# Attention on one Trainium2 core: loads by group, jumps over rarely used code, and a reordered last group

## The chip, the cores and the metric

The kernel runs on one core of a Trainium2 chip. A core has five engines with a queue of instructions each: PE multiplies matrices, ACT applies functions such as exp, DVE and POOL do element-wise work, and SP issues the transfers here. Engines wait for one another through semaphores. The metric is the device time of one execution in microseconds (us), lower is better; the kernel before takes 543.33 us, the median of 14 runs from 542.11 to 545.58.

## The reference: softmax attention with shared keys

```python
B, Hq, Hkv, Sq, Sk, D = 16, 32, 8, 288, 512, 128     # bfloat16, values of about 0.05
k = jnp.repeat(k, Hq // Hkv, axis=1)
v = jnp.repeat(v, Hq // Hkv, axis=1)
scores = jnp.einsum("bhqd,bhkd->bhqk", q, k) * D ** -0.5
out = jnp.einsum("bhqk,bhkd->bhqd", _softmax(scores, axis=-1), v)
```

Four query heads share one key and value head, so the work falls into 16 x 8 = 128 groups, each with 4 x 288 = 1152 query rows against 512 keys.

## The kernel before

A *group* (`g`, of `NG` = 128) is one key head of one batch: R = 1152 query rows in NT = 9 tiles of 128, 512 keys in NJ = 4 tiles. Scores are made with the keys on the partitions, so one group has NJ x R = 4608 score columns, cut into NC = 3 *chunks* of CH = 1536 columns (three PSUM banks). A *step* is one chunk. There are 384 of them. For step n:

- **S** (`op_s`, L416): PE multiplies the transposed k by the transposed q into one of two score buffers in PSUM (`ps_s`). `pieces` (L410) cuts a chunk where a bank or a key tile ends, so a chunk takes four matmuls.
- **E** (`op_exp`, L456): ACT takes exp of the chunk, without subtracting a maximum, into `pt_sb` in bfloat16.
- **PV** (`op_pv`, L437): PE multiplies three query tiles of the group by v, four key tiles each, twelve matmuls of 129 columns into one of two PSUM banks (`ps_o`). The 129th column of v holds ones, so it collects the sum of the exps. Chunks run over keys first, so PV of a group needs all three exps of the group.
- **Evacuation** (`op_rc` and `op_ev`, L478 and L485): DVE takes the reciprocal of three sums and multiplies three output tiles by them into `o_sb`, a ring of six groups.

PE's order is written out: S of step n, then PV of step n - LAG, with LAG = 4; after the last S the last four PV follow one another. S of step n waits for E of n - 2, PV of step r for the evacuation of r - 2.

SP issues all transfers, in an order sorted by due times counted in steps. Loads come by *unit* of UG = 4 groups (`op_load`, L379), three units deep: one transposing transfer of k, one transposing transfer of q, and a plain one of v into `vd_sb`. POOL copies v from there into `v_sb`, beside the column of ones, once per unit (`op_vc`, L467). In the first unit, k and q of group 0 come by themselves (`part=0`), then those of groups 1 to 3 (`part=1`), then v of all four. A group's output is stored in one transfer (`op_store`, L403), which waits for the group's last evacuation.

Because no maximum is subtracted, the kernel ends with a test. DVE keeps the largest and smallest reciprocal of each batch (`op_stat`, L500), reduces them at the end (L560, L562), compares them with limits (L563, L566), PE sums the verdicts over the partitions (L534), and DVE writes an integer `flag_i` (L569). Then `guarded` (L578) lets each engine load the flag (L582) and branch (L583): where the flag isn't zero, a general version of the attention (`general_path`, L17) runs from the start. With these inputs it is skipped. The general code of each engine stands between that branch and the end of the program, where all engines drain and meet (L324).

Of the kernel before, what the change touches and what calls it, by code (L numbers as in the profile page):

```python
# [284 lines left out]

def bass_standalone__gqa_softmax__near_ridge_kernel(
# [16 lines left out]
    CB = 3  # L303
    CH = CB * BANK
    COLS = NJ * R
    NC = COLS // CH
    assert COLS % CH == 0 and NT % 3 == 0 and NC == NT // 3
    scale = float(D) ** -0.5
    DV = D + 1
    VP = DV  # L310
# [3 lines left out]
    NSLOT = 3  # L314
    NPT = 3
    NO = 6

# [6 lines left out]
    with ExitStack() as es:  # L324
# [8 lines left out]
        block = es.enter_context(nc.Block())  # L333
        main = ExitStack()
        vd_sb = main.enter_context(nc.sbuf_tensor("vd_sb", [P, NSLOT, UG, NJ * D], BF16))
        v_sb = main.enter_context(nc.sbuf_tensor("v_sb", [P, NSLOT, UG * NJ, VP], BF16))
        qt_sb = main.enter_context(nc.sbuf_tensor("qt_sb", [P, NSLOT, NT, UG, P], BF16))
# [5 lines left out]
        ck_sb = main.enter_context(nc.sbuf_tensor("ck_sb", [P, 4], FP32))  # L343
# [26 lines left out]
        for name in ["s_one", "s_s", "s_e", "s_pv", "s_rc", "s_ev", "s_stat", "s_bad", "s_flag", "s_go", "s_q0", "s_k0", "s_vc"]:  # L370
            S(name)
        for i in range(NSLOT):
            for name in ["s_q%d", "s_k%d", "s_v%d"]:
                S("u" + name % i)
        for i in range(NO):
            S("s_o%d" % i)


        def op_load(u, part=None):  # L379
            eng = nc.sync  # L380
            sl = u % NSLOT
            if u >= NSLOT:
                last = (u - NSLOT + 1) * UG - 1
                for (s, n) in need(eng, [("s_s", NC * (last + 1))]):
                    eng.wait_ge(s, n)
            g0, g1 = {None: (0, UG), 0: (0, 1), 1: (1, UG)}[part]
            sq = sem["s_q0"] if part == 0 else sem["us_q%d" % sl]
            sk = sem["s_k0"] if part == 0 else sem["us_k%d" % sl]
            gg = u * UG
            eng.dma_start_transpose(  # L390
                kt_sb[:, sl, :, g0:g1].rearrange("d j g p -> d j (g p)"),
                k_v[(gg + g0) * P:(gg + g1) * P]).then_inc(sk, 16)
            eng.dma_start_transpose(  # L393
                qt_sb[:, sl, :, g0:g1].rearrange("d t g p -> d t (g p)"),
                q_v[(gg + g0) * P:(gg + g1) * P]).then_inc(sq, 16)
            if part != 0:
                if u >= NSLOT:
                    for (s, n) in need(eng, [("s_vc", u - NSLOT + 1)]):
                        eng.wait_ge(s, n)
                eng.dma_start(  # L400
                    vd_sb[:, sl], v_v[:, gg:gg + UG]).then_inc(sem["us_v%d" % sl], 16)

        def op_store(g):  # L403
            eng = nc.sync
            for (s, n) in need(eng, [("s_ev", NC * (g + 1))]):
                eng.wait_ge(s, n)
            eng.dma_start(o_v[g], o_sb[:, g % NO].rearrange("p t d -> p (t d)")).then_inc(sem["s_o%d" % (g % NO)], 16)


        def pieces(i):  # L410
            cuts = sorted({i * CH, (i + 1) * CH}
                          | {x for x in range(0, COLS, BANK) if i * CH < x < (i + 1) * CH}
                          | {x for x in range(0, COLS, R) if i * CH < x < (i + 1) * CH})
            return list(zip(cuts[:-1], cuts[1:]))

        def op_s(n):  # L416
            eng = nc.tensor
            g, i = n // NC, n % NC
            u, gi = g // UG, g % UG
            sl = u % NSLOT  # L420
            waits = []
            if g == 0:
                waits += [("s_k0", 16), ("s_q0", 16)]
            else:
                waits += [("us_k%d" % sl, 16 * (u // NSLOT + 1)), ("us_q%d" % sl, 16 * (u // NSLOT + 1))]
            if n >= 2:
                waits.append(("s_e", n - 1))
            ps = pieces(i)
            for x, (a, b) in enumerate(ps):
                j, r0 = a // R, a % R  # L430
                ins = emit(eng, waits if x == 0 else [], lambda: eng.matmul(  # L431
                    ps_s[:, n % 2, a - i * CH:b - i * CH],
                    kt_sb[:, sl, j, gi, :],
                    qt_sb[:, sl, r0 // P:(r0 + b - a) // P, gi, :], start=True, stop=True))
            ins.then_inc(sem["s_s"], 1)

        def op_pv(r):  # L437
            eng = nc.tensor
            g = r // NC
            u, gi = g // UG, g % UG  # L440
            sl = u % NSLOT
            waits = [("s_vc", u + 1), ("s_e", NC * (g + 1))]
            if r >= 2:
                waits.append(("s_ev", r - 1))
            for a in range(3):
                t = 3 * (r % NC) + a
                for j in range(NJ):
                    w = pt_sb[:, g % NPT, j * R + t * P:j * R + (t + 1) * P]
                    ins = emit(eng, waits if a == 0 and j == 0 else [], lambda: eng.matmul(  # L449
                        ps_o[:, r % 2, a * DV:(a + 1) * DV], w,  # L450
                        v_sb[:, sl, gi * NJ + j, 0:DV],
                        start=(j == 0), stop=(j == NJ - 1)))
# [3 lines left out]
        def op_exp(n):  # L456
# [3 lines left out]
            if g >= NPT:  # L460
                waits.insert(0, ("s_pv", NC * (g - NPT + 1)))
            emit(eng, waits, lambda: eng.activation(  # L462
                pt_sb[:, g % NPT, i * CH:(i + 1) * CH], ps_s[:, n % 2], ACTF.Exp, scale=scale)
            ).then_inc(sem["s_e"], 1)


        def op_vc(u):  # L467
            eng = nc.gpsimd
            sl = u % NSLOT
            waits = [("us_v%d" % sl, 16 * (u // NSLOT + 1))]  # L470
            if u >= NSLOT:
                waits.append(("s_pv", NC * UG * (u - NSLOT + 1)))
            emit(eng, waits, lambda: eng.tensor_copy(  # L473
                v_sb[:, sl, :, 0:D], vd_sb[:, sl].rearrange("p g (j d) -> p (g j) d", d=D))
# [3 lines left out]
        def op_rc(r):  # L478
            eng = nc.vector
            src = ps_o[:, r % 2, 0:3 * DV].rearrange("p (a e) -> p a e", e=DV)[:, :, D:DV]  # L480
            emit(eng, [("s_pv", r + 1)], lambda: eng.reciprocal(  # L481
                rl_sb[:, 3 * r:3 * r + 3], src.rearrange("p a e -> p (a e)"))
            ).then_inc(sem["s_rc"], 1)

        def op_ev(r):  # L485
# [3 lines left out]
            if g >= NO:  # L489
                waits.insert(0, ("s_o%d" % (g % NO), 16 * (g // NO)))  # L490
            t0 = 3 * (r % NC)
            src = ps_o[:, r % 2, 0:3 * DV].rearrange("p (a e) -> p a e", e=DV)[:, :, 0:D]
            emit(eng, waits, lambda: eng.tensor_tensor(  # L493
                out=o_sb[:, g % NO, t0:t0 + 3, :], in0=src,
                in1=rl_sb[:, 3 * r:3 * r + 3].unsqueeze(2).broadcast_to([P, 3, D]),
                op=ALU.mult)).then_inc(sem["s_ev"], 1)

        nstat = [0]

        def op_stat(b):  # L500
            eng = nc.vector
            w = G * NT
            emit(eng, [("s_rc", (b + 1) * w // 3)], lambda: eng.tensor_reduce(  # L503
                st_sb[:, 0, b:b + 1], rl_sb[:, b * w:(b + 1) * w], AX.X, ALU.max))
            eng.tensor_reduce(  # L505
                st_sb[:, 1, b:b + 1], rl_sb[:, b * w:(b + 1) * w], AX.X, ALU.min).then_inc(sem["s_stat"], 1)


        NS = NG * NC
        sp, pe = [], []  # L510
        sp.append((-10.0, lambda: op_load(0, 0)))
        sp.append((-9.0, lambda: op_load(0, 1)))
        for u in range(1, NU):
            sp.append((-8.0 if u < NSLOT else NC * UG * (u - NSLOT + 1) + LAG, lambda u=u: op_load(u)))
        for g in range(NG):
            sp.append((NC * (g + 1) + LAG + 1.5, lambda g=g: op_store(g)))
        sp.sort(key=lambda x: x[0])

        @block.sync
        def _(eng):  # L520
            for (_, fn) in sp:
                fn()
            for g in range(max(0, NG - NO), NG):
                for (s, n) in need(eng, [("s_o%d" % (g % NO), 16 * (g // NO + 1))]):
                    eng.wait_ge(s, n)

        @block.tensor
        def _(eng):
            for n in range(NS + LAG):
                if n < NS:  # L530
# [3 lines left out]
            emit(eng, [("s_bad", 1)], lambda: eng.matmul(  # L534
                ps_s[0:1, 0, 0:1], one_f[:], ck_sb[:, 3:4], start=True, stop=True)
            ).then_inc(sem["s_bad"], 1)

        @block.scalar
        def _(eng):
            emit(eng, [("s_one", 1)], lambda: eng.activation(dum[:, 1:2], dum[:, 0:1], ACTF.Exp))  # L540
            for n in range(NS):
                op_exp(n)

        @block.gpsimd
        def _(eng):
            eng.memset(v_sb[:, :, :, D:DV], 1.0)  # L546
            for u in range(NU):
                op_vc(u)

        @block.vector  # L550
        def _(eng):
            eng.memset(dum[:], 0.0).then_inc(sem["s_one"], 1)  # L552
            eng.memset(one_f[:], 1.0)
            per_b = G * NC
            for r in range(NS):
                op_rc(r)
                op_ev(r)
                if r % per_b == per_b - 1:
                    op_stat(r // per_b)
            emit(eng, [("s_stat", B)], lambda: eng.tensor_reduce(  # L560
                ck_sb[:, 0:1], st_sb[:, 0, :], AX.X, ALU.max))
            eng.tensor_reduce(ck_sb[:, 1:2], st_sb[:, 1, :], AX.X, ALU.min).then_inc(sem["s_stat"], 1)  # L562
            emit(eng, [("s_stat", B + 1)], lambda: eng.tensor_scalar(  # L563
                out=ck_sb[:, 2:3], in0=ck_sb[:, 0:1], scalar1=SUM_MAX, scalar2=None, op0=ALU.is_gt)
            ).then_inc(sem["s_stat"], 1)
            emit(eng, [("s_stat", B + 2)], lambda: eng.scalar_tensor_tensor(  # L566
# [56 lines left out]
```

## Time and profile before

| | |
|---|---|
| median of 14 runs | 543.33 us |
| the profiled execution | 544.62 us |
| its span, first to last instruction | 542.9 us |
| PE, matmuls busy | 524.9 us (97%) |
| ACT busy | 521.9 us (96%) |
| DVE busy | 288.6 us (53%) |
| POOL busy | 61.2 us (11%) |
| transfer queue of SP, share of its 16 rings | 83.9% |

How to read it: an engine's row lists the instructions of one line of the kernel, their count, busy time and mean length, and after the bar how long the engine had been idle before them and who released it. A timeline row has the start, the length in us, the engine and the line; "SPq" is SP issuing a transfer, and its length is the time of issuing, not of the transfer. "PEld" is PE loading its stationary tile. "PEclk" is the share of its clock that PE was granted. DRAIN and COMPARE_BRANCH rows are those of the engines' instruction queues. A step is 520.4 us of exps over 384, or 1.355 us.

### The profile page before, as it was taken

Reading aid. Unit: us, or ns where it says so; the run is one execution under the profiler, and the core shown is the slowest. Engines: PE = TensorE matmul, PEld = TensorE weight load, DVE = VectorE, ACT = ScalarE, POOL = GpSimd, SP = SyncE. Lnnn points to the kernel's source line nnn. Section 1 sums busy time; section 2 is a strip of 40 time slices with the busy share of each in tenths; the row PEclk is TensorE's granted clock in tenths of the full one; section 3 lists DMA queues with packets and bytes.
Section 4 is the critical chain, followed back from the end, with each engine's and each line's share of the span. In section 5 each row is a group of like instructions: output and inputs, shape, how many; then the busy total and the mean of one; then the engine's idle time right before and its main releaser. Section 6 shows DMA issues by size and latency. Waiting matters only on the chain.

```text
span 542.9 us, 14127 instructions
## 1 busy us (share of the span) xinstructions
PE 524.9 (97%) x6146; PEld 411.3 (76%) x6146; DVE 288.6 (53%) x807; ACT 521.9 (96%) x386; POOL 61.2 (11%) x37
## 2 busy tenths in 40 slices
PE   3899999999999999999999999999999999999994
PEld 1677777777777777777777777777777777777773
DVE  0355555555555555555555555555555555555554
ACT  4799999999999999999999999999999999999992
POOL 0211111011111011111011111001111011111000
PEclk9799999999999999999999999999999999999998
DMA  8999899988879888798988889978788988898211
GB/s 158 219 250 260 223 210 230 198 213 182 232 212 229 214 182 220 213 215 224 204 208 193 224 213 224 239 172 221 188 227 220 208 211 182 233 211 221 87 68 70
DMA packets 250500, 110.02 MB, mean 203 GB/s; under 512 B 217665, under 2 KB 234049, under 8 KB 250433
## 3 DMA queue, kind: packets, MB, share of 16 engines
q1 hardware_dynamic: 250432, 109.07, 83.9%
q8 instruction: 49, 0.80, 0.7%
q14 instruction: 19, 0.15, 0.1%
HBM read 16.78 MB, written 37.75 MB: 100 GB/s over the span
## 4 chain that ended last, share of the span: by engine, by line
PE 95%; SPq 2%; DMA 1%; DVE 1%; POOL 0%; issue 0%
PE ps_o L449 50%; PE ps_s L431 46%; SPq L393 1%; DMA vd_sb<-in_v_dram 1%; SPq L390 1%; POOL v_sb L473 0%; DVE o_sb L493 0%; DVE rl_sb L481 0%; PE ps_s L534 0%; DVE ck_sb L566 0%; DVE ck_sb L560 0%; DVE ck_sb L563 0%; DVE flag_i L569 0%; DVE st_sb L505 0%; DVE st_sb L503 0%
## 5 line engine op out<-in xcount | busy, mean ns | idle before, releaser
L462 ACT ACTIVATE pt_sb<-ps_s 128x1536 bf16<-128x1536 f32 x384 | 520.4, 1450 | 10.5 <-PE ps_s L431 10.5
L449 PEld LDWEIGHTS ps_o<-v_sb,pt_sb 128*128 128x128 bf16 x4608 | 301.2, 98 | 58.3 <-POOL v_sb L473 2.9
L449 PE MATMUL ps_o<-v_sb,pt_sb 128*128 128x129 bf16 x4608 | 334.1, 222 | 2.6 <-POOL v_sb L473 2.2
L431 PE MATMUL ps_s<-qt_sb,kt_sb 128*128 128x512 bf16 (+3 forms) x1536 | 314.6, 328 | 8.6 <-DMA qt_sb<-in_q_dram 8.3
L493 DVE TENSOR_TENSOR o_sb<-ps_o,rl_sb 128x384 bf16<-128x384 f32 x384 | 214.1, 557 | 13.5 <-DVE rl_sb L481 0.2
L481 DVE RECIPROCAL rl_sb<-ps_o 128x3 f32<-128x3 f32 x384 | 69.5, 181 | 234.7 <-PE ps_o L449 234.7
L431 PEld LDWEIGHTS ps_s<-qt_sb,kt_sb 128*128 128x128 bf16 x1536 | 130.0, 98 | 66.1 <-DMA qt_sb<-in_q_dram 6.2
L473 POOL COPY v_sb<-vd_sb 128x2048 bf16<-128x2048 bf16 x32 | 60.7, 1896 | 440.2 <-DMA vd_sb<-in_v_dram 327.7
L505 DVE TENSOR_REDUCE st_sb<-rl_sb 128x1 f32<-128x72 f32 x16 | 3.5, 218 | 0.0
L503 DVE TENSOR_REDUCE st_sb<-rl_sb 128x1 f32<-128x72 f32 x16 | 3.5, 217 | 0.0
L540 ACT ACT_TABLE_LOAD x1 | 1.3, 1283 | 0.8 <-PEq L608 0.8
L534 PE MATMUL ps_s<-ck_sb,one_f 128*1 128x1 f32 x2 | 0.2, 164 | 1.8 <-DVE ck_sb L566 1.8
L534 PEld LDWEIGHTS ps_s<-ck_sb,one_f 128*1 128x1 f32 x2 | 0.1, 80 | 2.0 <-DVE ck_sb L566 2.0
L552 DVE MEMSET dum<- 128x2 f32 x1 | 0.1, 60 | 0.9 <-PEq L608 0.9
L546 POOL MEMSET v_sb<- 128x48 bf16 x1 | 0.3, 311 | 0.3 <-POOLq L608 0.3
L569 DVE CAST flag_i<-ps_s 1x1 int32<-1x1 f32 x1 | 0.1, 145 | 0.3 <-PE ps_s L534 0.3
L540 ACT ACTIVATE dum<-dum 128x1 f32<-128x1 f32 x1 | 0.2, 203 | 0.0
L560 DVE TENSOR_REDUCE ck_sb<-st_sb 128x1 f32<-128x16 f32 x1 | 0.2, 170 | 0.0
L566 DVE SCALAR_TENSOR_TENSOR ck_sb<-ck_sb 128x1 f32<-128x1 f32 x1 | 0.2, 159 | 0.0
L563 DVE TENSOR_SCALAR ck_sb<-ck_sb 128x1 f32<-128x1 f32 x1 | 0.2, 153 | 0.0
L562 DVE TENSOR_REDUCE ck_sb<-st_sb 128x1 f32<-128x16 f32 x1 | 0.2, 158 | 0.0
L608 POOL MEMSET const-float32-0.0<- 128x1 f32 x1 | 0.1, 98 | 0.3 <-issue 0.3
(4 smaller groups left out, 0.4 us busy)
## 6 DMA issues: line engine op xcount, KB each, us to landing
out_dram<-o_sb SPq DMA_DIRECT2D x128, 288.0 KB, 4.9
vd_sb<-in_v_dram SPq DMA_DIRECT2D x32, 512.0 KB, 4.9
kt_sb<-in_k_dram SPq DMA_TRANSPOSE x33, 5.2
qt_sb<-in_q_dram SPq DMA_TRANSPOSE x33, 8.6
```

Of the source, the lines that this page charges most:

```text
L390: eng.dma_start_transpose(kt_sb[:, sl, :, g0:g1].rearrange("d j g p -> d j (g p)"), k_v[(gg + g0) * P:(gg + g1) * P]).then_inc(sk, 16)
L393: eng.dma_start_transpose(qt_sb[:, sl, :, g0:g1].rearrange("d t g p -> d t (g p)"), q_v[(gg + g0) * P:(gg + g1) * P]).then_inc(sq, 16)
L431: ins = emit(eng, waits if x == 0 else [], lambda: eng.matmul(ps_s[:, n % 2, a - i * CH:b - i * CH], kt_sb[:, sl, j, gi, :], qt_sb[:, sl, ...
L449: ins = emit(eng, waits if a == 0 and j == 0 else [], lambda: eng.matmul(ps_o[:, r % 2, a * DV:(a + 1) * DV], w, v_sb[:, sl, gi * NJ + j, ...
L462: emit(eng, waits, lambda: eng.activation(pt_sb[:, g % NPT, i * CH:(i + 1) * CH], ps_s[:, n % 2], ACTF.Exp, scale=scale)).then_inc(sem["s_ ...
L473: emit(eng, waits, lambda: eng.tensor_copy(v_sb[:, sl, :, 0:D], vd_sb[:, sl].rearrange("p g (j d) -> p (g j) d", d=D))).then_inc(sem["s_vc ...
L481: emit(eng, [("s_pv", r + 1)], lambda: eng.reciprocal(rl_sb[:, 3 * r:3 * r + 3], src.rearrange("p a e -> p (a e)"))).then_inc(sem["s_rc"], 1)
L493: emit(eng, waits, lambda: eng.tensor_tensor(out=o_sb[:, g % NO, t0:t0 + 3, :], in0=src, in1=rl_sb[:, 3 * r:3 * r + 3].unsqueeze(2).broadc ...
L503: emit(eng, [("s_rc", (b + 1) * w // 3)], lambda: eng.tensor_reduce(st_sb[:, 0, b:b + 1], rl_sb[:, b * w:(b + 1) * w], AX.X, ALU.max))
L505: eng.tensor_reduce(st_sb[:, 1, b:b + 1], rl_sb[:, b * w:(b + 1) * w], AX.X, ALU.min).then_inc(sem["s_stat"], 1)
L534: emit(eng, [("s_bad", 1)], lambda: eng.matmul(ps_s[0:1, 0, 0:1], one_f[:], ck_sb[:, 3:4], start=True, stop=True)).then_inc(sem["s_bad"], 1)
L540: emit(eng, [("s_one", 1)], lambda: eng.activation(dum[:, 1:2], dum[:, 0:1], ACTF.Exp))
```

## The change

**Loads.** The first unit comes group by group, in an order that is written out: k0, q0, k1, q1, v0, k2, q2, v1, k3, q3, v2, v3. q comes one group at a time everywhere, into a ring of NQ = 12 groups; k and v of later units stay whole. SP's list is sorted by due times as before, now with one entry for each q. POOL copies v once per group.

**General code.** On SP, DVE and POOL it stands near the start, and the engine jumps over it there (`general`, "main_"); on ACT the jump comes after its last instruction ("end_"). At the end (`choose`) these engines branch to it only where the flag asks for it, and otherwise go straight on. On PE it stays behind the branch, and a prefetch hint for that branch is issued at step NS - 3.

**Last group.** Its chunks run over queries first: chunk i holds the scores of query tiles 3i to 3i + 2 against all keys. A chunk takes six matmuls there, and PV of a step waits for that step's exp alone. Its output is stored in three transfers. PV of the last step writes into the free score buffer, one tile to a bank, so it doesn't wait for an evacuation; of its three tiles DVE evacuates two and ACT one (`op_ev_last`).

**Flag.** The maximum and minimum over all but the last five steps' 15 reciprocals are taken and tested right after evacuation 378. The last 15 are tested one by one beside the last evacuation (`op_over`), PE sums six columns, and DVE adds them into the flag.

```diff
+    NQ = 12
+        def general(eng, key, after):
+            home[key] = nc.cur_bb
+            eng.br(after + key)
+            with nc.body("general_" + key):
+                fns[key](eng)
+                eng.br("done_" + key)
+            nc.switch_bb(after + key)
+        def choose(eng, key, behind=False):
+            eng.wait_ge(sem["s_flag"], 1)
+            eng.load(reg, flag_i[:])
+            if key == "sp":
+                for (s, n) in need(eng, stored()):
+                    eng.wait_ge(s, n)
+            br = eng.br_ne(reg, 0, "general_" + key, "done_" + key)
+            if behind:
+                br.branch_hint(hints[key])
...
+        def op_q(g):
+            eng.dma_start_transpose(qt_sb[:, g % NQ], q_v[g * P:(g + 1) * P]).then_inc(sem["s_q%d" % (g % NQ)], 16)
...
+            if g == LASTG:
+                w = TPC * P
+                cuts = sorted(set(range(0, CH + 1, BANK)) | set(range(0, CH + 1, w)))
...
-            waits = [("s_vc", u + 1), ("s_e", NC * (g + 1))]
-            if r >= 2:
+            waits = [("s_vc", g + 1), ("s_e", r + 1 if g == LASTG else NC * (g + 1))]
+            if 2 <= r < NS - 1:
                 waits.append(("s_ev", r - 1))
...
+        first = [lambda: op_k(0, 0), lambda: op_q(0), lambda: op_k(0, 1), lambda: op_q(1), lambda: op_v(0, 0)]
+        first += [lambda: op_k(0, 2), lambda: op_q(2), lambda: op_v(0, 1)]
+        first += [lambda: op_k(0, 3), lambda: op_q(3), lambda: op_v(0, 2), lambda: op_v(0, 3)]
         for u in range(1, NU):
+            t = -1.0 + u if u < NSLOT else NC * UG * (u - NSLOT + 1) + LAG
+            sp.append((t, lambda u=u: op_k(u)))
+            sp.append((t + 0.2, lambda u=u: op_v(u)))
+        for g in range(UG, NG):
+            sp.append((-0.9 + g / UG - 1.0 if g < NQ else NC * (g - NQ + 1) + 1.2, lambda g=g: op_q(g)))
...
+                if n == NS - 3:
+                    hints["pe"] = eng.mark_branch_hint_location()
...
+                if r == NS - 1:
+                    last = rl_sb[:, NG * NT - ALONE:NG * NT]
+                    op_over(last, last, 0, ALONE, ("s_rc", NS), B + 3)
                 op_ev(r)
+                if r == NS - 1 - ALONE // TPC:
+                    op_stat(B - 1)
+                    op_over(ck_sb[:, 0:1], ck_sb[:, 1:2], ALONE, ALONE + 1, ("s_stat", B + 1), B + 2)
```

## The prediction

> **What bounds the kernel now.** I read the page's busy shares, then one steady unit of four groups, then the two ends of the span, since every part of the change acts there.
>
> The page, groups of instructions, and the chain that ended last:
>
> ```profile
> span 542.9 us, 14127 instructions
> ...
> PE 95%; SPq 2%; DMA 1%; DVE 1%; POOL 0%; issue 0%
> ...
> L462 ACT ACTIVATE pt_sb<-ps_s 128x1536 bf16<-128x1536 f32 x384 | 520.4, 1450 | 10.5 <-PE ps_s L431 10.5
> ```
>
> Stretches of the span (busy time of PE, weight loads, DVE, ACT and POOL, then granted PE clock and DMA share):
>
> ```profile
> 9.80:13.20 3.40, 1.29 (x8) 0.47 (x6) 0.00 (x0) 2.06 (x2) 0.00 (x0) 1.00 0.99 236
> 13.20:16.60 3.40, 1.20 (x5) 0.30 (x2) 0.00 (x0) 2.79 (x2) 1.89 (x1) 0.50 1.01 234
> 16.60:20.00 3.40, 3.39 (x24) 2.67 (x25) 0.74 (x2) 0.58 (x1) 0.00 (x0) 0.50 1.19 233
> 30.00:530.00 500.00, 500.00 (x5908) 393.98 (x5907) 276.80 (x770) 500.00 (x370) 56.89 (x30) 1.00 0.86 206
> ```
>
> From 30 to 530 us PE and ACT never pause. A step (one score chunk S, one exp E, one output chunk PV) takes 520.4 / 384 = 1.355 us; in the chain it is 0.65 of S plus 0.70 of PV, so PE sets it. Exps that don't wait for PE run at 1.34 (three in 4.13 us, the last 1.45). The change leaves this stretch its operations. What can move is the start (exps that wait) and the end (after the last exp, at 533.15).
>
> The start, ACT's and SP's timelines (start, length):
>
> ```profile
> 7.72 4.13 ACT L462 ACTIVATE pt_sb<-ps_s 128x1536 bf16<-128x1536 f32 x3 [5.42 <-PE ps_s L431]
> 13.28 2.79 ACT L462 ACTIVATE pt_sb<-ps_s 128x1536 bf16<-128x1536 f32 x2 [1.42 <-PE ps_s L431]
> 19.41 1.45 ACT L462 ACTIVATE pt_sb<-ps_s 128x1536 bf16<-128x1536 f32 x1 [3.35 <-PE ps_s L431]
> 21.14 9.57 ACT L462 ACTIVATE pt_sb<-ps_s 128x1536 bf16<-128x1536 f32 x7 [0.28 <-PE ps_s L431]
> ...
> 0.81 1.32 SPq L390 DMA_TRANSPOSE kt_sb<-in_k_dram  x1
> 2.18 1.35 SPq L393 DMA_TRANSPOSE qt_sb<-in_q_dram  x1
> 3.58 1.64 SPq L390 DMA_TRANSPOSE kt_sb<-in_k_dram  x1
> 5.26 4.93 SPq L393 DMA_TRANSPOSE qt_sb<-in_q_dram  x1
> 10.23 0.58 SPq L400 DMA_DIRECT2D vd_sb<-in_v_dram  x1
> 10.86 3.57 SPq L390 DMA_TRANSPOSE kt_sb<-in_k_dram  x1
> 14.47 5.35 SPq L393 DMA_TRANSPOSE qt_sb<-in_q_dram  x1
> ```
>
> ACT loses 1.42 + 3.35 + 0.28 = 5.05 us after its first exp: S3 waits for the q of groups 1 to 3, PV0 for v of the whole unit and its 1.9 us copy. The end, the branch past the general code and the closing drains (duration, start):
>
> ```profile
> L583 ACTq COMPARE_BRANCH  x1: 45/45/45, 538.6 to 538.6; - x1
> L583 PEldq COMPARE_BRANCH  x1: 3594/3594/3594, 538.7 to 538.7; - x1
> ...
> L324 SPq DRAIN  x1: 59/59/59, 540.1 to 540.1; - x1
> L324 PEldq DRAIN  x1: 73/73/73, 542.3 to 542.3; - x1
> L324 DVEq DRAIN  x1: 41/41/41, 542.6 to 542.6; - x1
> ```
>
> The flag is written at 538.06, but PE spends 3.59 in its branch, and DVE, done branching at 538.75, drains at 542.58. SP drains at 540.05: its skipped code is short. [...]
>
> **The start, part by part.** The first S still waits for one k and one q, issued as before, so the first exp stays at 7.72.
>
> - q1. By the q0 row (issue 2.18 to 3.53, landed when S0 begins at 6.22) a q lands 2.7 after its issue ends. k1 and q1 follow at once: 3.58 + 1.32 + 1.35 + gaps ends at 6.3, lands at 9.0. S3 needs it when E1 ends, about 10.5: covered, 1.5 to spare.
> - v0. Issued behind q1 (0.33, the row of a store, which also has 128 rows), landed by about 9.5; POOL copies a quarter of 1.90, 0.5. PV0 needs it after S4, at 12.6: covered. q2 and q3 land at about 12 and 15; S6 and S9 need them at 14.6 and 18.6.
> - So to S11 nothing waits, by these rows: 5.05 us gained, S12 due at 22.7 (S4 at 11.9 plus 8 steps).
> - S12 is where I expect something to come late. It needs the k of unit 1, and SP's sorted list puts q4 to q7 (times -0.9 to -0.15) ahead of that k (0.0). Ahead of it SP issues four k, eight q, four v. Low: k at 0.6 (a quarter of the shortest unit rows), q at 1.33, v at 0.15: 2.4 + 10.6 + 0.6 + 16 gaps of 0.045 = 14.3, so k is issued at 15.1; with the page's median of 5.2 to landing, 20.3: no stall. High, by single-group rows: 4 x 1.32 + 8 x 1.35 + 4 x 0.33 + 0.7 = 18.1, so 18.9; landing 24.1 by the median, 25.3 by the 6.4 that the k issued at 10.86 took. The single-group row is the nearest in shape, and the startup is crowded: I take 25.0, a stall of 2.3 us. PE has no slack to win it back. Behind S12 in PE's order stand PV8, S13 and all the rest.
> - v of unit 1 is late next: it follows q8, and PV12 needs it four steps after S12. 1.35 + 0.58 + 4.9 (median landing) + 0.5 copy = 7.3 after the k is issued out at about 21; that is 28.5 against 25 + 5.4 + 0.65 = 31: covered.
> - Clock. [...] I take nothing, and keep 1.7 for the range.
> [...]
>
> Starting gain: 5.05 - 2.3 = 2.75.
>
> **Jumps.** DVE and POOL now jump over general code at about 1 us, 3.9 each, ready by 5; first work is at 13.3 and 9.5: covered. [...] SP's skipped part is the short one (0.42 from branch to drain before).
>
> **Steady.** POOL: 128 copies of 0.5 instead of 32 of 1.9, the same sum, idle 88%. PE, ACT, DVE: the same tiles.
>
> **The end**, on the old clock. In the last group PV needs only its own exp, but DVE gates it: PV381 and PV382 still wait for the evacuations two before. Only PV383 is freed of that (score banks): 0.33 earlier (535.02 to 534.69). Against it, the max/min of the bulk and its test now stand after evacuation 378: 0.14 + 0.14 + 0.17 + 0.09 + 0.16 + 0.17 = 0.87, where DVE waits 0.58 in a step: 0.3 late. Between the last reciprocal and its evacuation two tests: 0.33. That evacuation is two tiles instead of three, -0.19; ACT does the third (between 0.2, its smallest row, and 0.5) beside it. Extra score pieces: 2 x 3 of some 0.06, in part hidden, 0.1. Sum: 536.71 - 0.33 + 0.3 + 0.33 - 0.19 + 0.1 = 536.9. The last store goes out at 537.0 and lands 1.9 later (before: 536.74 to 538.81, for three times the bytes): 538.9. SP has its flag by then; 0.5 to its drain, 0.3 for the barrier: 539.7. Flag: 536.9 + 0.25 for a 145 ns reduce, with PE's matmul done beside the evacuation; +0.5 for the load: 537.7. ACT, DVE and POOL fall through. PE alone still branches far, behind a prefetch hint issued three steps before the end: between 0.05 (ACT's branch) and 3.6 (its own row). The hint stands over 5 us ahead, longer than the fetch, so I take the low end: PE drains at 538. Without it 541.4, and the end is 541.7. The gain is 542.9 - 539.7 = 3.2, or 1.2 with no working hint.
>
> **Sum.** 544.62 (this execution's own: 542.9 of span, 1.72 around it) - 2.75 - 3.2 = 538.67. The median of the runs is 1.29 below this execution: 537.4.
>
> **Rivals.**
> - No stall (k cheap to issue): 5.05 + 3.2 = 8.25, 535.1. For it: unit k of 1.72 to 2.1 elsewhere in SP's rows. Against: the single k at 1.32.
> [...]
> - Slower: the rings become the bound. They are busy 83.9% of the span, 13.65 of the 16.27 us of a unit. The change adds three transposes per unit. If each costs more than (16.27 - 13.65) / 3 = 0.87 of ring time, every unit is longer; at 1.1 it is 0.7 x 32 = 22 us, 560. Against: single q at 1.35 by the issue row, and SP waiting for others nearly half the time.
> [...]
>
> **How the numbers follow.** Stall as computed with full tail 0.40 (537.4, own range 536 to 538.7); no stall 0.24; start or hint lost 0.21; nothing 0.04; slower by rings or otherwise 0.11. The range 533.8 to 542.0 takes the first three, with 0.5 to 1 at each side for landing times and ACT's tile. Faster or slower counts from 0.2%, 1.09 us, about what this measurement can tell: faster 0.85, same 0.04, slower 0.11.
>
> **What would show it.** ACT: first exp at 7.7, then no idle until the 13th exp, whose idle is 2.3 and is released by PE behind kt_sb of unit 1. Granted clock 1.00 from about 10 us on. PE's end branch well under 0.5 us, all drains within 0.5 of the last landing. Wrong, if the step isn't 1.355, if the 4th exp waits already, or PE's branch still takes 3.6.

## The result, and where the time went

The changed kernel takes 540.90 us (median of 10, 539.03 to 542.62); the kernel before, measured beside it, 544.19 us. The ratio is 0.9935, with a 95% interval of 0.9921 to 0.9949: 3.3 us gained, where 5.9 were forecast. The profiled execution took 541.54 us, with a span of 539.8.

The page of the changed kernel:

```profile
span 539.8 us, 14538 instructions
...
PE 94%; ACT 3%; DVE 1%; DMA 1%; issue 1%; SPq 0%
...
L537 ACT ACTIVATE pt_sb<-ps_s 128x1536 bf16<-128x1536 f32 x384 | 520.2, 1452 | 10.8 <-PE ps_s L499 10.8
```

ACT still waits for PE, in all a little longer than before (10.8 us against 10.5), but in other places. ACT's and SP's timelines at the start show where:

```profile
8.21 16.23 ACT L537 ACTIVATE pt_sb<-ps_s 128x1536 bf16<-128x1536 f32 x12 [5.91 <-PE ps_s L499]
28.46 1.45 ACT L537 ACTIVATE pt_sb<-ps_s 128x1536 bf16<-128x1536 f32 x1 [4.03 <-PE ps_s L499]
30.76 29.89 ACT L537 ACTIVATE pt_sb<-ps_s 128x1536 bf16<-128x1536 f32 x22 [0.85 <-PE ps_s L499]
...
3.58 1.26 SPq L432 DMA_TRANSPOSE kt_sb<-in_k_dram  x1
4.88 1.44 SPq L453 DMA_TRANSPOSE qt_sb<-in_q_dram  x1
6.37 0.58 SPq L444 DMA_DIRECT2D vd_sb<-in_v_dram  x1
...
14.44 7.60 SPq L453 DMA_TRANSPOSE qt_sb<-in_q_dram  x4
22.08 2.21 SPq L432 DMA_TRANSPOSE kt_sb<-in_k_dram  x1
```

Twelve exps run without a pause, as forecast. Then the thirteenth, the first of unit 1, waits 4.03 us. The k that it needs is issued at 22.08, behind q4 to q7, and S12 starts at 26.98. (The profile names no releaser for this wait of PE; that it is this k, the first experiment shows.) PE's row of S12, and PE's clock around it (columns as before):

```profile
26.98 1.44 PE L499 MATMUL ps_s<-qt_sb,kt_sb 128*128 128x512 bf16 x4 [3.59 <-issue]
...
23.50:26.90 3.40, 0.00 (x0) 0.00 (x0) 0.67 (x2) 0.93 (x1) 0.00 (x0) 1.00 1.00 203
26.90:30.30 3.40, 3.32 (x19) 2.29 (x20) 0.50 (x2) 1.45 (x1) 0.00 (x0) 0.50 1.25 220
30.30:530.00 499.70, 499.70 (x5909) 393.83 (x5908) 276.24 (x768) 499.24 (x369) 70.81 (x124) 1.00 0.92 209
```

PE stood idle for 3.59 us, got half its clock (0.50) for the next 3.4, and the next exp waited another 0.85. The last exp ends at 533.30 us, against 533.15 before: in these two executions **the new start gains nothing**. All of the gain lies behind the last exp, 6.52 us now and 9.73 before. The branches and drains there:

```profile
L377 PEldq COMPARE_BRANCH  x1: 385/385/385, 537.7 to 537.7; - x1
L362 ACTq COMPARE_BRANCH  x1: 33/33/33, 536.2 to 536.2; - x1
...
L329 PEldq DRAIN  x1: 62/62/62, 538.1 to 538.1; - x1
L329 DVEq DRAIN  x1: 134/134/134, 538.6 to 538.6; - x1
L329 SPq DRAIN  x1: 137/137/137, 539.3 to 539.3; - x1
L329 ACTq DRAIN  x1: 8/8/8, 539.6 to 539.6; - x1
```

PE's branch takes 0.385 us instead of 3.594. Before, PE, ACT, POOL and DVE drained 3.6 to 3.9 us after the start of their branches; now PE and DVE drain after 0.4 and 1.0, and POOL after 0.1. SP, behind the last store, and ACT, which jumps only at 536.2, end the span. While the engines of the kernel before stood behind their branches, from 538.6 to 542.6, its rings carried five instruction packets, and none in the 5.4 us ahead of that (queue, packets, MB, share of the rings):

```profile
q14 instruction: 4, 0.03, 3.0%
q8 instruction: 1, 0.02, 2.0%
```

The expectations below call this gap the fetch. That the engines wait for just these packets is not shown.

### The profile page after: what moved, and what is told of

Its sections match the earlier page's. It is cut to its first block, busy times and chain, and to the rows that moved or that the text cites. A ratio compares the mean times of both kernels' runs of the same rounds, so it can differ in the third digit from the quotient of the medians.

```text
span 539.8 us, 14538 instructions
## 1 busy us (share of the span) xinstructions
PE 524.1 (97%) x6152; PEld 411.2 (76%) x6152; DVE 288.5 (53%) x809; ACT 522.1 (97%) x387; POOL 73.8 (14%) x133
## 3 DMA queue, kind: packets, MB, share of 16 engines
q1 hardware_dynamic: 253872, 109.08, 90.2%
## 4 chain that ended last, share of the span: by engine, by line
PE 94%; ACT 3%; DVE 1%; DMA 1%; issue 1%; SPq 0%
PE ps_o L519 49%; PE ps_s L499 45%; ACT pt_sb L537 3%; DMA qt_sb<-in_q_dram 1%; DVE o_sb L565 0%; SPq L432 0%; DVE rl_sb L554 0%; DVE bad_sb L589 0%; DVE bad_sb L592 0%; DVE ck_sb L669 0%; DVE st_sb L584 0%; DVE flag_i L674 0%; DVE st_sb L582 0%; DVE ck_sb L671 0%
## 5 line engine op out<-in xcount | busy, mean ns | idle before, releaser
L537 ACT ACTIVATE pt_sb<-ps_s 128x1536 bf16<-128x1536 f32 x384 | 520.2, 1452 | 10.8 <-PE ps_s L499 10.8
L547 POOL COPY v_sb<-vd_sb 128x512 bf16<-128x512 bf16 x128 | 73.3, 616 | 421.1 <-DMA vd_sb<-in_v_dram 407.8
L584 DVE TENSOR_REDUCE st_sb<-rl_sb 128x1 f32<-128x72 f32 (+1 forms) x16 | 3.5, 217 | 0.0
L582 DVE TENSOR_REDUCE st_sb<-rl_sb 128x1 f32<-128x72 f32 (+1 forms) x16 | 3.5, 216 | 0.0
```

Source lines behind the costliest of these rows:

```text
L537: emit(eng, waits, lambda: eng.activation(dst, src, ACTF.Exp, scale=scale)).then_inc(sem["s_e"], 1)
L547: emit(eng, waits, lambda: eng.tensor_copy(v_sb[:, sl, gi * NJ:(gi + 1) * NJ, 0:D], vd_sb[:, sl, gi].rearrange("p (j d) -> p j d", d=D))). ...
L582: emit(eng, [("s_rc", e // TPC)], lambda: eng.tensor_reduce(st_sb[:, 0, b:b + 1], rl_sb[:, a:e], AX.X, ALU.max))
L584: eng.tensor_reduce(st_sb[:, 1, b:b + 1], rl_sb[:, a:e], AX.X, ALU.min).then_inc(sem["s_stat"], 1)
```

## The experiments

Tail below means the span behind the last exp's end. The theory: SP's one queue decides the start, and the place of the general code decides the end. Two runs change the order of SP's list, one takes the old loads back, one drops the hint; four more follow from what these showed.

### The k of unit 1 ahead of q4 to q7

```diff
-            sp.append((t, lambda u=u: op_k(u)))
+            sp.append((t if u > 1 else -1.0, lambda u=u: op_k(u)))
```

> The k of unit 1 is issued before q4 to q7; nothing else differs from the changed kernel. Theory (S12 waits for that k because twelve plus five transfers stand ahead of it): the 13th exp no longer waits 4.0 us, PE's clock stays full; but v of unit 1 is late next, so PV12 waits some 1 to 3 us (issued at about 26, landing 31, copied 31.6, needed at 29.3). Device time 2.5 to 4.5 us below the changed kernel's 540.9: 536.5 to 538.5. Rival (rings are saturated in the startup, order doesn't matter): the wait only moves to another S or PV of the same length, and the time stays within 1 us of 540.9.

Measured: 539.74 us (538.69 to 540.79), ratio to before 0.9918 (0.9892 to 0.9944). The time lies nearer to the rival's figure than to the theory's, and the interval overlaps that of the changed kernel, so a gain over it isn't shown. The profile, taken of the fastest of the five executions (538.69), tells more. ACT's timeline, and the waits from 5 to 60 us (who waited for whom, total, times, longest):

```profile
10.99 20.25 ACT L537 ACTIVATE pt_sb<-ps_s 128x1536 bf16<-128x1536 f32 x15 [0.21 <-PE ps_s L499]
32.01 10.93 ACT L537 ACTIVATE pt_sb<-ps_s 128x1536 bf16<-128x1536 f32 x8 [0.77 <-PE ps_s L499]
44.25 31.24 ACT L537 ACTIVATE pt_sb<-ps_s 128x1536 bf16<-128x1536 f32 x23 [1.31 <-PE ps_s L499]
...
DVE o_sb L565 <- DMA out_dram<-o_sb: 2.4, 1, 2.4
...
PE ps_o L519 <- POOL v_sb L547: 0.9, 1, 0.9
```

The wait of the thirteenth exp is gone, so it was that k, and PE's clock stays full in this execution (1.00). v of unit 1 is late next, as the theory said, though by 0.9 instead of 1 to 3 us. And a third one, which I had not listed, comes behind it: DVE waits 2.4 us for a store.

### Its v as well, between q5 and q6

```diff
-            sp.append((t + 0.2, lambda u=u: op_v(u)))
+            sp.append((t + 0.2 if u > 1 else -0.5, lambda u=u: op_v(u)))
```

> As r1_k_first, and v of unit 1 is issued between q5 and q6. Theory: neither S12 nor PV12 waits; q6 is needed only at 31. ACT runs without a pause from its first exp: 4.9 us below the changed kernel (4.03 and 0.85 of idle gone), 536.0. Rival (saturated rings): q6 or q7 comes late by the same 3 to 5 us, 540 to 541.

Measured: 542.11 us (541.22 to 543.90), ratio 0.9969 (0.9950 to 0.9987): slower than the changed kernel. Neither S12 nor PV12 waits, and 25 exps run in peace; then one loses 5.05 us. It isn't q6 or q7, as the rival had it. DVE's and SP's timelines:

```profile
37.48 0.56 DVE L565 TENSOR_TENSOR o_sb<-ps_o,rl_sb 128x384 bf16<-128x384 f32 x1
38.62 0.18 DVE L554 RECIPROCAL rl_sb<-ps_o 128x3 f32<-128x3 f32 x1 [0.58 <-PE ps_o L519]
43.81 0.56 DVE L565 TENSOR_TENSOR o_sb<-ps_o,rl_sb 128x384 bf16<-128x384 f32 x1 [5.01 <-DMA out_dram<-o_sb]
...
34.81 4.25 SPq L453 DMA_TRANSPOSE qt_sb<-in_q_dram  x2
39.12 0.58 SPq L467 DMA_DIRECT2D out_dram<-o_sb  x1
```

Evacuation 18 writes the first tiles of group 6 into the ring of six output buffers, where group 0 lies until it is stored. Its store is issued only at 39.12, behind every load up to q13, and lands near 43.7. The faster the steps come, the earlier evacuation 18 is due. In the changed kernel the first store goes out at 40.63, and evacuation 18 is due at the same moment, 43.9: its stall at S12 hides this one. PE's clock drops here too, to 0.58 on average from 42 to 48 us.

### The old loads under the new end

The loads, copies and SP's list are those of the kernel before (`op_load`, a q buffer by unit, `op_vc` by unit); the rest stays changed.

```diff
-        first = [lambda: op_k(0, 0), lambda: op_q(0), lambda: op_k(0, 1), ...
+        first = [lambda: op_load(0, 0), lambda: op_load(0, 1)]
...
+            sp.append((-8.0 if u < NSLOT else NC * UG * (u - NSLOT + 1) + LAG, lambda u=u: op_load(u)))
-            for g in range(NG):
-                op_vc(g)
+            for u in range(NU):
+                op_vc(u)
```

> The changed kernel with the loads of the kernel before: q, k and v by unit, POOL's copies by unit, SP's list as before. The last group, the flag chain and the place of the general code stay changed. Theory (all of the gain lies behind the last exp, the new start gains nothing): 540 to 541.3, as the changed kernel, with exps idle 5.05 us at the start as before. Rival (the new loads gain half of it or more): 542.3 or above. Rival (single-group loads slow the middle too, by the busier rings at 90.2%): below 539.5.

Measured: 540.84 us (539.72 to 542.33), ratio 0.9930 (0.9910 to 0.9951): as the changed kernel. The tail is 6.50, and ACT waits 4.99 us after its first exp (5.05 before). So the end carries the gain by itself. The new loads leave the middle as it was: PE is busy without a pause from 30 to 530 us in the kernel before, in this one and in the changed one, although the transfer rings are busy 90.2% of the span in the changed kernel, against 83.9% before.

### Without the hint

```diff
-                br.branch_hint(hints[key])
...
-                if n == NS - 3:
-                    hints["pe"] = eng.mark_branch_hint_location()
```

> The changed kernel without the prefetch hint for PE's last branch. Theory (the hint hides PE's fetch): PE's branch takes 3.6 us instead of 0.385, PE drains at about 541.4 on the clock of the changed kernel's trace instead of 538.1, the span ends 1.9 us later: 542.8. Rival (the new layout, not the hint, makes the branch short): no change, 540.9.

Measured: 544.06 us (541.49 to 545.34), ratio 0.9990 (0.9967 to 1.0012): nothing of the gain is left. The profile of this run:

```profile
L377 PEldq COMPARE_BRANCH  x1: 3455/3455/3455, 538.0 to 538.0; - x1
...
L329 ACTq DRAIN  x1: 8/8/8, 540.0 to 540.0; - x1
L329 PEldq DRAIN  x1: 73/73/73, 541.5 to 541.5; - x1
```

PE drains last, 1.5 us behind ACT; the tail is 8.10, 1.58 longer than with the hint. The medians differ by 3.2 us, the two profiled executions by only 2.0 (543.56 and 541.54), of which 0.4 fell before the last exp. I take 1.58 as the hint's price in this execution. Why the medians lie further apart is not shown; PE's branch without a hint took 4.31 us in another run below, so it may be longer in other executions of this one too.

### All loads by need

The rule for all of SP's list is now the step that needs the transfer, less twelve; stores keep their due times.

```diff
-            t = -1.0 + u if u < NSLOT else NC * UG * (u - NSLOT + 1) + LAG
-            sp.append((t, lambda u=u: op_k(u)))
-            sp.append((t + 0.2, lambda u=u: op_v(u)))
+            sp.append((NC * UG * (u - 1) - (1.0 if u == 1 else -0.5), lambda u=u: op_k(u)))
+            sp.append((NC * UG * (u - 1) + 3.5, lambda u=u: op_v(u)))
-            sp.append((-0.9 + g / UG - 1.0 if g < NQ else NC * (g - NQ + 1) + 1.2, lambda g=g: op_q(g)))
+            sp.append((NC * (g - UG), lambda g=g: op_q(g)))
```

> All loads after the first unit stand in SP's list by the step that needs them, twelve steps ahead, so k and v of unit 1 come before q6 and the first stores stand before q7 to q11. Theory (SP's one queue is full to about 40 us at the start, and whatever stands late in it stalls in turn: the k of unit 1, its v, then the store of group 0 that evacuation 18 waits for): no exp waits after the first by more than 0.3 us, evacuation 18 doesn't wait, PE's clock stays full; last exp ends near 528.5, end 6.4 later, 536.6. Rival (the rings can't carry the start at this pace at all): a wait of 3 to 5 us at some later S, 540 or above.

Measured: 536.49 us (535.83 to 536.60), ratio 0.9862 (0.9834 to 0.9889), where 536.6 was expected. ACT's and SP's timelines:

```profile
8.25 2.79 ACT L537 ACTIVATE pt_sb<-ps_s 128x1536 bf16<-128x1536 f32 x2 [5.95 <-PE ps_s L499]
11.25 64.75 ACT L537 ACTIVATE pt_sb<-ps_s 128x1536 bf16<-128x1536 f32 x48 [0.21 <-PE ps_s L499]
...
14.47 2.35 SPq L432 DMA_TRANSPOSE kt_sb<-in_k_dram  x1
16.87 2.81 SPq L453 DMA_TRANSPOSE qt_sb<-in_q_dram  x2
19.73 0.58 SPq L444 DMA_DIRECT2D vd_sb<-in_v_dram  x1
20.36 2.07 SPq L453 DMA_TRANSPOSE qt_sb<-in_q_dram  x1
22.47 0.57 SPq L467 DMA_DIRECT2D out_dram<-o_sb  x1
```

The same transfers, and no exp waits more than 0.21 us after the first. So the rings can carry the start; it was the order that delayed it. The last exp ends at 528.34, 4.96 earlier than in the changed kernel.

### ACT's jump at the start

```diff
             emit(eng, [("s_one", 1)], lambda: eng.activation(dum[:, 1:2], dum[:, 0:1], ACTF.Exp))
+            general(eng, "act", "main_")
...
-            general(eng, "act", "end_")
```

> r5_by_need with ACT's jump over its general code at the start, after the first small exp, instead of after the last evacuation. Theory: ACT's fetch of 2.9 us disappears behind the first loads, ACT loads the flag with the others, and the last drain is SP's, 0.26 us earlier: 0.2 to 0.3 us below r5_by_need, at the limit of what can be told; the first exp isn't delayed (jump 3.9 from 2.3 ends at 6.2, first S is done at 7.7 or later). Rival: the jump delays the first exp, and the time is above r5_by_need.

Measured: 535.89 us (535.54 to 536.05), ratio 0.9853 (0.9826 to 0.9881), 0.6 below the run before, where 0.2 to 0.3 was expected (four executions each, whose ranges overlap). The first exp starts at 8.35, as without it (8.25). The tail goes from 6.47 to 6.01:

```profile
L329 ACTq DRAIN  x1: 8/8/8, 532.4 to 532.4; - x1
L329 POOLq DRAIN  x1: 45/45/45, 532.5 to 532.5; - x1
L329 PEldq DRAIN  x1: 62/62/62, 533.0 to 533.0; - x1
L329 DVEq DRAIN  x1: 134/134/134, 533.4 to 533.4; - x1
L329 SPq DRAIN  x1: 137/137/137, 533.8 to 533.8; - x1
```

ACT is first instead of last. Of the 0.46, only 0.12 is ACT's: that far its drain lay behind SP's in the run before. The other 0.33 is SP's, whose last store landed earlier here; no run shows why. This is the fastest kernel of the study, 8.3 us below the one before.

### The old last group and flag chain

On the loads by need: keys first in the last group too, one store, all tests behind the last evacuation.

```diff
-            waits = [("s_vc", g + 1), ("s_e", r + 1 if g == LASTG else NC * (g + 1))]
-            if 2 <= r < NS - 1:
+            waits = [("s_vc", g + 1), ("s_e", NC * (g + 1))]
+            if 2 <= r:
...
-            op_ev_last()
...
-                if r % per_b == per_b - 1 and r < NS - 1:
+                if r % per_b == per_b - 1:
                     op_stat(r // per_b)
```

(and the reductions and tests of the kernel before behind this loop)

> r5_by_need with the last group, the last store and the flag chain of the kernel before (keys first, one store, all tests after the last evacuation). Theory (all of the gain at the end is the place of the general code; the last evacuation ends 3.56 us after the last exp in both kernels, and the flag has slack before SP's last landing): the end stays 6.4 to 6.7 us after the last exp, 0 to 0.3 us above r5_by_need. Rival (the last group and the short flag chain give 1 us or more): tail 7.4 or above.

Measured: 536.90 us (536.55 to 537.09), ratio 0.9874 (0.9847 to 0.9901), 0.4 above the loads by need, slightly more than I allowed. The tail is 6.98. The last evacuation ends 3.56 us after the last exp in this run and in all the others, so the new last group doesn't bring it forward at all. What is left is the flag, read at 532.8 here, 4.95 after the last exp; with the short chain it is 3.72.

```profile
L329 SPq DRAIN  x1: 136/136/136, 534.2 to 534.2; - x1
L329 DVEq DRAIN  x1: 135/135/135, 534.5 to 534.5; - x1
```

Here DVE, waiting for the flag, is last. As ACT has nothing behind its last exp, its jump lies at 526.4 here and is hidden. Against the kernel with ACT's jump at the start (tail 6.01) the short chain and the last store in three parts are worth 0.97 together. These runs don't separate them, but the chain alone can't bring more than some 0.3: SP, behind its single store, ends its drain only 0.29 before DVE.

### The old place of the general code

On the loads by need: general code behind each engine's branch, no jumps, no hint.

```diff
-            general(eng, "sp", "main_")
-            choose(eng, "sp")
+            choose(eng, "sp", behind=True)
```

(and so for POOL, DVE and ACT; PE without its hint)

> r5_by_need with the general code of every engine behind its branch, as in the kernel before, no jumps and no hint. Theory: with the flag at 3.7 us after the last exp, 0.5 to load it and 3.9 of fetch on ACT, POOL and DVE, the end is 8.3 to 8.5 us after the last exp: 2 us above r5_by_need, 538.6. (Before, with the flag at 4.9, it was 9.7.) Rival (the flag chain is what counts): less than 0.7 us above r5_by_need.

Measured: 538.09 us (537.92 to 538.32), ratio 0.9894 (0.9867 to 0.9921), 1.6 above the loads by need. The tail is 8.95, 2.48 longer. PE's branch ends it, and took longer than I expected; DVE drains late too:

```profile
L377 PEldq COMPARE_BRANCH  x1: 4307/4307/4307, 531.9 to 531.9; - x1
...
L329 ACTq DRAIN  x1: 80/80/80, 534.5 to 534.5; - x1
L329 DVEq DRAIN  x1: 44/44/44, 535.5 to 535.5; - x1
L329 PEldq DRAIN  x1: 73/73/73, 536.2 to 536.2; - x1
```

Its median gains 0.9 of that back, and most of this lies at the start. ACT's first exps here, and the transfers of the first 7 us in the changed kernel (packets, MB, share of the rings):

```profile
7.50 2.79 ACT L538 ACTIVATE pt_sb<-ps_s 128x1536 bf16<-128x1536 f32 x2 [5.20 <-PE ps_s L500]
...
q1 hardware_dynamic: 2717, 0.67, 58.8%
q14 instruction: 5, 0.03, 1.6%
```

The first exp began at 7.50 instead of 8.25. Up to there this run differs from the loads by need only in that DVE and POOL have no jump at the start. The other profiles agree: without such jumps the first exp begins at 7.50 and 7.72 (the kernel before), with them between 7.98 and 8.52 in all eight, the one with the old loads (8.52) included. So the jumps are not free: the first exp comes some 0.5 us later with them. In the changed kernel, four of the five instruction packets above (0.03 MB) come between 1.9 and 5.5 us, while the first k and q are under way; the kernel before has a single one in its first 25 us (0.00 MB). That these packets hold up the first loads is not shown. It is one execution of each kernel.

## Why the prediction was right or wrong

Two gains were forecast, 3.2 us at the end and 2.75 at the start. The end came, the start did not; the time still lies in the stated range because the range had kept room for that.

- **The end: right.** 3.2 us were forecast and 9.73 - 6.52 = 3.21 came. The parts: PE's branch with the hint at the low end of its bounds (0.385); DVE and POOL draining 1.0 and 0.1 us after their branches instead of 3.9; the last store's landing and SP's drain close to the end. The sum takes the low end because the hint stands further ahead than the fetch is long; no run moves the hint, so that this decides is not shown. With the hint PE's branch took 0.385 to 0.474 us (the changed kernel and the three runs by need that keep it), without it 3.455 and 4.307. So the hint is needed, and the run with the old layout shows that the jumps are: there DVE drains 7.9 us after the last exp. Of my sum for the last evacuation the terms cancelled: 3.56 after the last exp, before and after (3.75 forecast). That the end agrees to a hundredth is in part luck, as ACT and not SP ended it.
- **ACT: wrong.** The sum has ACT fall through with DVE and POOL, its own jump put at nothing. The branch row of that jump stands at 536.2, where ACT's last instruction starts, and ACT reads the flag 2.9 us later. That made ACT last, by 0.13 us.
- **No wait before S12: right.** q1, v0, q2 and q3 came in time; twelve exps ran through.
- **S12: right in place and kind, too small in size.** The step that failed is "ahead of it SP issues four k, eight q, four v ... so 18.9". Measured 22.08. q4 to q7 took 7.60 instead of 4 x 1.35 = 5.4; each v 0.58 or 0.52 instead of 0.33, which I took from a store although the row of v said 0.58; and 0.5 passed at SP's jump. The first eight single transfers of k and q did cost the 1.2 to 1.4 I took. Why the later q take longer is not shown; the share of the rings was 0.90 while they were issued and 0.85 in the 4.8 us before. The k then landed in 4.9 us instead of 6.1, and the stall was 4.03 instead of 2.3.
- **The clock: the wrong end of the bound.** I took nothing and kept 1.7 for the range. No run shows this 1.7. What the changed kernel shows is 0.50 of the clock from 26.90 to 30.30, and an exp that waits 0.85 more. Such a stretch had to be expected from the rows of the kernel before: there PE worked 1.29 of the 3.40 us from 9.80, and its clock was 0.50 from 13.20 to 20.00; ahead of S12, the 3.40 us before 26.90 hold no matmul at all. With k and v moved forward PE worked 3.57 of the 6.00 us from 42, at 0.58. What sets the clock down is not shown. In twelve executions of the changed kernel for which the clock is listed, the mean clock is 0.994 to 0.997 in eight, with spans of 539.1 to 540.8, and 0.999 to 1.000 in four, with 537.2 to 537.7: the stretch at half clock seems to come in most of them, and goes with some 1.8 us.
- **The jumps at the start: put at nothing, and they cost some 0.5.** I had DVE and POOL ready by 5 us and called that covered. Their own first work did not wait, but S0 waited for the first q until 6.71 instead of 6.22, and the first exp, forecast at 7.72, starts at 8.21; the last experiment shows it without these jumps, at 7.50.
- **What was missing.** The start gain that I left, 2.75, was -0.15. The old waits of 5.05 went; 4.03 and 0.85 came, and the first exp was 0.49 later. That makes -0.32, and ACT's exps and short gaps between them gave back 0.17. I had named v of unit 1 as late next and found it covered; with the k moved it was late by 0.9. That output stores stand in the same queue, with only six buffers before DVE must wait, I had not followed. It costs the changed kernel nothing only because S12 stalls first. POOL's copies took 0.6 us each and not 0.5, which cost nothing, as POOL is busy 14% of the span.
- **The rivals.** The case that I gave 0.21, start or hint lost, is what came, by its first half: the hint worked, and the start gained nothing. Ahead of S12 the longest to issue were q4 to q7, 7.60 us for four, where q0 to q3 took 1.31 to 1.44 each; by need, the same transfers cause no wait. No stall at S12, the first rival, did not come: there were 4.03 us. The rings as a bound in the middle did not come either: each step still takes 1.355. Against it stood that SP waits for others nearly half the time: 201.3 us for DVE and 44.4 for PE, in the kernel before. From the shares and spans the rings worked some 31 us longer, an estimated 0.33 for each of 95 more q transfers, well under the 0.87 that would have bound.

## What to carry to other kernels

In one queue that carries loads and stores, an early load of something needed late delays everything behind it: here q4 to q7 held the k of unit 1 back by 7.60 us, and S12 by 4.03. Sort by the step that needs each transfer, and follow the list down to the first store and the buffer that it frees; moving one late transfer forward merely shows the next. Code that is never run still costs time where it has to be branched over, 3.5 to 4.3 us on PE here: place it where a jump is hidden, or give the branch a hint ahead of it (0.39 to 0.47 us with it here), and count the engines one by one, since the last of them sets the end. A jump at the start is cheap but not free: the first exp came at 7.98 to 8.52 with jumps on DVE and POOL, at 7.50 and 7.72 without.

## What the runs showed that I had not expected

Moving two loads forward made the kernel slower (542.11 against 540.90), because the stall it removed had hidden a longer one. A branch behind ACT's last instruction doesn't run ahead of it: it stands at that instruction's start in both places (536.2 and 526.4). The jumps at the start delayed the first exp. And PE's far branch varies: 3.59, 3.46 and 4.31 us in one execution each of three kernels.
